# A two-layer spectral mixer and MLP: folded row halves, permuted weights in the second layer, w4 in the order table, and table loads on another queue

## The chip, the cores and the metric

The kernel runs on one core of one Trainium2 chip. The metric is the device time of one execution in microseconds (us). In this kernel TensorE does the matmuls, into banks of the memory called PSUM; ScalarE and VectorE copy and combine the results into the on-chip memory SBUF; GpSimd computes small statistics; SyncE issues loads and stores. All executions compared here are fast (mean granted TensorE clock 0.99 to 1.0). A profile gives the span of one execution, mostly 1.7 to 2.0 us shorter than its time; positions below are us from the start of the span. Line numbers (L403) belong to the kernel whose profile is shown, so the same instruction has another number in the changed kernel.

## The reference, cut to what matters

```python
def A(x):                      # spectral layer, x is [2048, 512]
    X = rfft2(x) * (w_r + 1j * w_i)
    return irfft2(X).astype(bfloat16)

def B(x):                      # mixer and MLP
    h  = gelu(layernorm(x) @ w1)
    hs = concat(h's four column groups, shifted by -1, +1, -2, +2 rows) @ w2
    x1 = x + hs
    return x1 + gelu(layernorm(x1) @ w3) @ w4

x = x + A(layernorm(x));  x = x + B(layernorm(x))     # layer 1
x = x + A(layernorm(x));  x = x + B(layernorm(x))     # layer 2
```

The transforms are matrix products with tables. In each layer: a transform over row groups ("front", into V), a forward DFT over columns (d), one over rows (q), the weighting (p, z), and the inverse steps b, D and P; then w1, w2, w3, w4.

## The kernel before

Each letter of the order table calls one small function; `d4` runs `over_d(4)`, `t4` runs `take_d(4)`, and so on. A schedule is thus a string, and in the timelines every engine runs its own instructions in that order. The code is cut, and `...` marks a cut.

```python
def over_p(K, qs):                      # front: rows' halves added and subtracted by TensorE
    ...
            K.nc.tensor.matmul(o, lhsT=K.x[:, q, a:a + P], rhs=Tq[:, 0:1].to_broadcast([P, 2, P]), start=True, stop=False)
            K.nc.tensor.matmul(o, lhsT=K.x[:, q, z:z + P], rhs=Tq[:], start=False, stop=True)

def take_d(u):                          # t: PSUM -> TV, every second element written
        copy_act(K, tv[u][:].rearrange("p n (e f h) -> p n h e f", e=2, h=2),
                 ps.pop(("d", u)).rearrange("p n (h e f) -> p n h e f", e=2, h=2))

def take_q(u):                          # x: PSUM -> X, two buffers
        X[u] = K.stream.tile([P, 2, 512], BF16, name="X", bufs=2)
        copy_act(K, X[u][:, 0:len(UNITS[u])], ps.pop(("q", u)))

def weigh(u):                           # p: two products on VectorE
    ...
            nc.vector.tensor_tensor(t[:, 0:n], x, w, op=ALU.mult)

def weigh2(u):                          # z: difference and sum on VectorE
        nc.vector.tensor_tensor(z[:, :, 0], a[:, :, 0], b[:, :, 1], op=ALU.subtract)
        nc.vector.tensor_tensor(z[:, :, 1], a[:, :, 1], b[:, :, 0], op=ALU.add)

def take_b(b, eng):                     # m: PSUM -> M, on VectorE ("V") or ScalarE ("A")
```

The 16 column blocks are taken as six pairs and four single units. PSUM has two banks for d, two for q and four for b during this stage. The w4 rows, the layer-norm statistics for layer 2 and the front of layer 2 were issued by plain loops after the order table.

## Time and profile before

| | value | where it is read |
|---|---|---|
| time | 384.94 us, median of 4 (384.69 to 385.62) | the runs |
| span | 383.4 us | the page's first line |
| TensorE's streaming time, from columns | 345.6 us | worked out in the prediction |
| spectral stage of layer 1, of layer 2 | 27.44, 26.87 us | the windows view |
| end of layer 1's w4 to layer 2's first DFT matmul | 5.55 us | the windows view |

The columns of the windows view are: the window, its length, then for PE, PEld, DVE, ACT and POOL the busy us with the number of instructions in brackets, then the clock, the DMA share and GB/s. I cut it at landmarks, which splits the span into pieces that must add up, so that each later difference has a place.

### The profile page before, as it was taken

To read this page: it belongs to the slowest core of one execution; us is meant where nothing else is said; L and a number is where in the kernel's file an instruction comes from. 1 tells how busy PE (TensorE), PEld (TensorE's weight loads), DVE (VectorE), ACT (ScalarE), POOL (GpSimd) and SP (SyncE) were. 2 spreads that over 40 slices of the span, in tenths; PEclk is the share of its full clock that TensorE was granted. 3 is DMA by queue.
4 is the path that set the end of the run, shared out by engine and by line. 5 is a ranking of instruction groups with operands and counts; after the bars stand their busy time and mean duration, and the time that the engine had idled before them with its cause. 6 is when DMAs were issued, how large, how long until landed. Compare 5 with 4: busy or idle time off the path is not lost.

```text
span 383.4 us, 5555 instructions
## 1 busy us (share of the span) xinstructions
PE 354.7 (93%) x2144; PEld 198.7 (52%) x2144; DVE 184.6 (48%) x461; ACT 214.7 (56%) x327; POOL 67.2 (18%) x162
## 2 busy tenths in 40 slices
PE   0869889999999999999996998999999999999996
PEld 0646678445554444444555676855555444444442
DVE  4829969639730321503743996983873011020122
ACT  5768968976987034051225896988598703405100
POOL 3700008443500010000210000753351000000000
PEclk9999999999999999999999999999999999999999
DMA  7945940000000000000000000000000000010011
GB/s 266 328 119 124 358 137 3 0 2 1 3 0 2 0 0 2 0 0 2 0 3 0 0 2 0 2 3 1 2 0 2 0 27 29 0 41 15 27 41 44
DMA packets 12666, 15.17 MB, mean 40 GB/s; under 512 B 1120, under 2 KB 10336, under 8 KB 12640
## 3 DMA queue, kind: packets, MB, share of 16 engines
q1 hardware_dynamic: 11776, 11.34, 9.4%
q10 hardware_dynamic: 864, 3.47, 2.7%
q8 instruction: 17, 0.28, 0.3%
q14 instruction: 9, 0.07, 0.1%
HBM read 12.71 MB, written 2.10 MB: 39 GB/s over the span
## 4 chain that ended last, share of the span: by engine, by line
PE 80%; ACT 8%; DMA 6%; DVE 3%; issue 1%; SPq 1%; POOL 1%; ACTq 0%; DVEq 0%; POOLq 0%
PE ps L555 25%; PE ps L579 25%; PE ps L518 6%; PE ps L502 6%; PE ps L446 4%; ACT TV L145 3%; PE ps L480 3%; PE ps L434 3%; PE ps L372 3%; DMA W<-in_A_w_r_dram 2%; DMA TL<-tab_TL 2%; DMA x_state<-in_A_x_dram 1%; PE ps L416 1%; ACT X L145 1%; PE ps L417 1%
## 5 line engine op out<-in xcount | busy, mean ns | idle before, releaser
L562 ACT ACTIVATE gT<-ps 128x1024 bf16<-128x1024 f32 x56 | 56.9, 1024 | 77.4 <-PE ps L555 77.2
L579 PE MATMUL ps<-w,gT 128*128 128x512 bf16 x448 | 98.3, 379 | 1.4 <-ACT gT L562 1.4
L555 PE MATMUL ps<-xT,w 128*128 128x512 bf16 x448 | 99.0, 379 | 0.0
L581 DVE TENSOR_TENSOR x_state<-ps,x_state 128x512 bf16<-128x512 f32 x32 | 22.1, 691 | 136.7 <-PE ps L579 136.7
L579 PEld LDWEIGHTS <-gT 128*128 128x128 bf16 x448 | 43.7, 98 | 54.3 <-ACT gT L562 2.4
L555 PEld LDWEIGHTS <-w 128*128 128x128 bf16 x448 | 43.5, 98 | 51.0
L145 ACT ACTIVATE xT<-ps 128x1024 bf16<-128x1024 bf16 x32 | 32.1, 1024 | 9.4 <-PE ps L480 9.4
L208 DVE BATCH_NORM_STATS2 ln_st<-x_state 128x6 f32<-128x512 bf16 x43 | 29.4, 683 | 5.1 <-DMA x_state<-in_A_x_dram 4.6
L526 DVE SCALAR_TENSOR_TENSOR xn<-xn,ln_c,ps 128x512 bf16<-128x512 bf16 x32 | 23.2, 744 | 16.2 <-PE ps L518 15.6
L518 PE MATMUL ps<-w,hT 128*128 128x512 bf16 x128 | 29.5, 379 | 0.1
L502 PE MATMUL ps<-xT,w 128*128 128x512 bf16 x128 | 28.8, 379 | 0.0
L145 ACT ACTIVATE V<-ps 128x1024 bf16<-128x1024 f32 (+1 forms) x13 | 12.0, 977 | 28.1 <-PE ps L276 26.8
L274 PE MATMUL ps<-Tq,x_state 128*128 128x256 bf16 x64 | 16.0, 292 | 12.3 <-DVE Tq L263 11.9
L403 DVE TENSOR_TENSOR Pab<-X,W 128x1024 bf16<-128x1024 bf16 (+1 forms) x40 | 21.6, 579 | 11.6 <-DMA W<-in_A_w_i_dram 6.3
L224 POOL TENSOR_SCALAR ln_mv<-ln_s 128x4 f32<-128x4 f32 (+2 forms) x21 | 6.6, 313 | 116.2 <-ACT junk L219 115.6
L145 ACT ACTIVATE TV<-ps 128x1024 bf16<-128x1024 f32 (+1 forms) x20 | 21.5, 1087 | 6.9 <-PE ps L372 6.9
L219 ACT ACTIVATE junk<-xn 128x512 bf16<-128x512 bf16 x32 | 19.9, 623 | 6.2 <-DVE xn L526 6.2
L372 PE MATMUL ps<-FA,V 128*128 128x256 bf16 x128 | 16.9, 272 | 5.6 <-ACT TV L145 3.0
L233 POOL TENSOR_TENSOR ln_r<-ln_ve,mhalf 128x4 f32<-128x4 f32 (+1 forms) x19 | 18.3, 961 | 13.9 <-DVE ln_ve L232 12.7
L518 PEld LDWEIGHTS <-hT 128*128 128x128 bf16 x128 | 12.3, 98 | 14.2 <-ACT hT L509 0.8
L502 PEld LDWEIGHTS <-w 128*128 128x128 bf16 x128 | 12.3, 98 | 14.0 <-issue 0.3
L145 ACT ACTIVATE Y<-ps 128x1024 bf16<-128x1024 f32 x16 | 15.9, 1021 | 5.8 <-PE ps L434 3.0
(65 smaller groups left out, 436.9 us busy)
## 6 DMA issues: line engine op xcount, KB each, us to landing
w<-in_B_w_dram SPq DMA_DIRECT2D x2, 1792.0 KB, 12.3
x_state<-in_A_x_dram SPq DMA_DIRECT2D x8, 256.0 KB, 5.6
out_dram<-x_state SPq DMA_DIRECT2D x16, 128.0 KB, 1.8
TL<-tab_TL ACTq DMA_DIRECT2D x2, 768.0 KB, 7.1
TR<-tab_TR ACTq DMA_DIRECT2D x2, 768.0 KB, 7.8
w<-in_B_w_dram SPq DMA_DIRECT2D x2, 512.0 KB, 5.1
W<-in_A_w_r_dram SPq DMA_DIRECT2D x12, 64.0 KB, 2.7
W<-in_A_w_i_dram SPq DMA_DIRECT2D x12, 64.0 KB, 2.3
```

Of the source, the lines that this page charges most:

```text
L145: K.nc.scalar.activation(dst, src, ACT.Copy, bias=0.0, scale=1.0)
L208: v.bn_stats(st[:], src)
L219: K.nc.scalar.activation(junk[:], src, ACT.Square, bias=0.0, scale=1.0, accum_out=self.s[:, i, 1:2])
L372: nc.tensor.matmul(o[:, i, (1 - h) * 256:(2 - h) * 256], rhs=K.FA[:, t, h], lhsT=V[:, 2 * t + h, b].rearrange("d q c -> d (q c)"), start=( ...
L403: nc.vector.tensor_tensor(t[:, 0:n], x, w, op=ALU.mult)
L502: nc.tensor.matmul(o[:, i], lhsT=K.w1[:, t, j * P:(j + 1) * P], rhs=xT[g][:, t, :], start=(t == 0), stop=(t == 3))
L518: nc.tensor.matmul(o, lhsT=K.hT[:, j, st:st + P], rhs=K.w2[:, j, :], start=(j == 0), stop=(j == 3))
L526: nc.vector.scalar_tensor_tensor(xn[:, q, :], xn[:, q, :], ln[q // 4].c[:, q % 4:q % 4 + 1], ps.pop(("u", n)), op0=ALU.mult, op1=ALU.add, ...
L555: nc.tensor.matmul(o[:, i], lhsT=K.w3[:, c, t * P:(t + 1) * P], rhs=xT3[g][:, c, :], start=(c == 0), stop=(c == 3))
L562: nc.scalar.activation(gT[g][:, 2 * j:2 * j + 2, :], ps.pop(("w", k)), ACT.Gelu_apprx_tanh, bias=0.0, scale=1.0)
L579: nc.tensor.matmul(o, lhsT=gT[g][:, t, i * P:(i + 1) * P], rhs=K.w4[:, t, :], start=(t == 0), stop=(t == 13))
L581: nc.vector.tensor_tensor(K.x[:, q, :], o, K.x[:, q, :], op=ALU.add)
```

## The change

Its intent: take columns off TensorE, cheapen ScalarE's copy in the second spectral stage, fill TensorE's stalls by a finer order, and get the weights in sooner. The core of the diff:

```diff
-    loads = {5: ("TL", slice(0, 8)), 8: ("TR", slice(0, 8)), 11: ("TL", slice(8, 16)), 14: ("TR", slice(8, 16))}
+    loads = {5: ("TL", slice(0, 8)), 8: ("TR", slice(0, 8))}
 ...                                     # load_all, after the first half of W on SyncE
+        if lo == 0:
+            K.load_q("TL", slice(8, 16), nc.sync)
+            K.load_q("TR", slice(8, 16), nc.sync)
 ...
+def over_p_plain(K, qs):                 # front for five of the pairs of rows
+        for t in range(4):
+            K.nc.tensor.matmul(ps[:, i, t * P:(t + 1) * P], lhsT=K.x[:, q, t * P:(t + 1) * P], rhs=Tq[:, 0], start=True, stop=True)
+def fold_V(K, qs, ps, right):            # right: the right halves, copied to SBUF by ScalarE
+    for h, op in ((0, ALU.add), (1, ALU.subtract)):
+        for t in range(2):
+            K.nc.vector.tensor_tensor(v[:, h, t], left[:, t], right[:, t], op=op)
 ...
+        if last:
+            copy_act(K, tv[u][:], src)   # layer 2: folded order, a plain copy
+        else:
+            copy_act(K, tv[u][:].rearrange("p n (e f h) -> p (n e) h f", e=2, h=2), src.rearrange(...))
+def permute(k):                          # weights to folded order, 8 times, in layer 1's order
+        nc.vector.tensor_copy(tw.rearrange("p b (h f) -> p b h f", h=2), w.rearrange("p b (f h) -> p b h f", h=2))
+        nc.vector.tensor_copy(w, tw)
 ...                                     # G is loaded again, with permuted rows, between the layers
-    for op in ORDER.split():             # then loops for w4 and the front
+    for op in (ORDER_B if last else ORDER_A).split():   # w4, its addition, statistics, stores and the front are letters too
```

Less visible: both order tables are new throughout, the spectral part included, and m13 moved from ScalarE to VectorE. The order also moves one pair of the front's rows from ahead of layer 1's last w4 row to behind it. The second step of the layer-norm statistics is issued in a batch, and d's columns stand in another order in PSUM.

## The prediction

> **What bounds the kernel now.** I read the page's busy shares first, then the chain of work that ended last, then the busy time of each engine between landmarks that I took from that chain, and last the timeline around each place where TensorE stood still.
>
> ```profile
> PE 354.7 (93%) x2144; PEld 198.7 (52%) x2144; DVE 184.6 (48%) x461; ACT 214.7 (56%) x327; POOL 67.2 (18%) x162
> ...
> PE 80%; ACT 8%; DMA 6%; DVE 3%; issue 1%; SPq 1%; POOL 1%; ACTq 0%; DVEq 0%; POOLq 0%
> ```
>
> TensorE carries 80% of the chain. Its 93% is inflated, since pipelined matmuls overlap in the record. The chain gives the real pitch: "16 L555 in 3.45 us" is 0.216 us for 512 columns, and 16 transposes of 128 columns in 0.89 us are 0.0556 us each. I counted columns. The groups with 512 columns (L555 448, L579 448, L518 128, L502 128, L390 32) are 1184 matmuls. Those with 256 (L372, L446 and L434 at 128 each; L274, L276, L416, L417 at 64; L388, L389 at 32) are 704, or 352 units of 512. The 256 transposes are 64. So 1600 units at 0.216 us, 345.6 us of the 383.4. Only the 38 us in which TensorE does not stream can go, unless columns go.
>
> Where they lie comes from the windows view, cut at landmarks: first forward-DFT matmul (21.58 in layer 1, 206.15 in layer 2), first inverse-DFT matmul (49.02, 233.02), first w3 (96.79, 279.66), w4 (124.76, 307.63), end of w4 (200.62, 379.93). The columns are window, length, then busy us of PE, PEld, DVE, ACT, POOL.
>
> ```profile
> 21.58:49.02 27.44, 22.96 (x177) 16.91 (x177) 20.72 (x47) 22.68 (x30) 0.00 (x0) 1.00 0.67 204
> 49.02:96.79 47.77, 47.07 (x337) 29.40 (x338) 34.09 (x93) 38.78 (x74) 19.93 (x50) 1.00 0.06 21
> 124.76:200.62 75.86, 75.86 (x369) 36.05 (x370) 26.61 (x62) 18.21 (x18) 5.60 (x9) 1.00 0.00 1
> 200.62:206.15 5.53, 3.55 (x32) 2.88 (x30) 4.27 (x9) 2.43 (x3) 0.55 (x1) 1.00 0.00 0
> 206.15:233.02 26.87, 22.84 (x177) 16.97 (x177) 20.72 (x47) 22.70 (x30) 0.00 (x0) 1.00 0.00 1
> ```
>
> Each spectral stage needs 96 units, 20.7 us, and takes about 27. The w3/w4 stretches are full. The boundary between the layers (200.62 to 206.15) is a serial chain. These lines of the DVE timeline show what paces the spectral stage:
>
> ```profile
> 210.86 0.76 DVE L403 TENSOR_TENSOR Pab<-X,W 128x512 bf16<-128x512 bf16 x2 [4.76 <-ACT X L145]
> ...
> 213.87 1.28 DVE L403 TENSOR_TENSOR Pab<-X,W 128x1024 bf16<-128x1024 bf16 x2
> 215.19 0.42 DVE L409 TENSOR_TENSOR Z<-Pab 128x512 bf16<-128x512 bf16 x1
> 215.53 0.42 DVE L410 TENSOR_TENSOR Z<-Pab 128x512 bf16<-128x512 bf16 x1
> 216.23 1.29 DVE L403 TENSOR_TENSOR Pab<-X,W 128x1024 bf16<-128x1024 bf16 x2 [0.29 <-ACT X L145]
> ...
> 231.59 1.28 DVE L425 CAST M<-ps 128x512 bf16<-128x512 f32 x2
> ```
>
> The reader is to see that VectorE waits 4.76 us for its first X and then hardly stops until the last M. A pair of units costs it 2.0 us (two products, two sums, starts at 213.87 and 215.87), plus 0.6 for each M copy. So this stage is a late start plus 20 us of VectorE, not ScalarE's, though ScalarE is busier in sum. And each layer has one stall before w4:
>
> ```profile
> 306.35 0.59 PE L579 MATMUL ps<-w,gT 128*128 128x512 bf16 x2
> 307.63 2.55 PE L579 MATMUL ps<-w,gT 128*128 128x512 bf16 x11 [0.68 <-ACT gT L562]
> ```
>
> **What the Trainium skill says.** TensorE: Matmul & The Clock Gate, section "Wait — 56ns, not 53.3ns?": warm matmuls start every N ÷ 2.4 GHz plus about 2.5 ns, 55.6 ns at 128 and 215.7 at 512. The trace agrees (0.0556, 0.216). Halved columns are really half the time. VectorE: DVE Perf Modes, section "The perf-mode tier table": a tensor_tensor with a PSUM operand runs at one element per cycle; its errata section gives (N+151)/0.96 ns for fp32. The 512-element add from PSUM (L581) takes 691 ns, as that says; a fold of 256 elements should take 424. ScalarE: Activation LUTs, section "What ACT_TABLE_LOAD costs": 186 + 0.833·N ns, with back-to-back overlap of about 93. That is 1039 for N = 1024; X takes 1012, so it agrees, but TV, the same size written with every second element skipped, takes 1318, which the page doesn't have. DMA: Bandwidth & Descriptors, section "Issuing engines are not separate DMA queues": a second issuer saves only issue time. Here an issue costs SyncE 0.55 to 0.60 us and ScalarE 0.33.
>
> **The change part by part.**
>
> 1. Row halves folded on VectorE. For five of the pairs of rows ahead of layer 2 the sum and difference of the halves no longer come from TensorE (four 256-column matmuls per row) but from four of 128 columns, then an add and a subtract. Ten rows times 4 × (0.109 − 0.0556) = −2.15 us, in a stretch where TensorE has no gap: full value. VectorE gets 20 folds at some 0.35 pitch (0.42 less overlap), 7 us, and loses two casts (1.8). It was busy in 12 of the 19 us from 187 to 206, so it fits, if tightly.
>
> 2. The boundary. Before, 5.53 us from the last w4 to the first DFT matmul. In the new order the last row (E = end of w4) is: add to E+0.7, statistics to 1.65, GpSimd about 0.9 meanwhile one fold set to 3.0, table Tq 3.3, matmuls 3.9, ScalarE copy 4.5, while VectorE folds again to 4.65 and copies the last quarter by 5.05. So 5.05: −0.5. The TensorE work in this gap (3.4 us) is as before.
>
> 3. Layer 2's TV in folded order, with the weights permuted and G reloaded to match. TV becomes a plain copy: 6 × (1.32 − 1.02) + 4 × (0.74 − 0.61) = 2.3 us off ScalarE. Most of it is off the path. What counts is when VectorE starts its stream of pairs: before at 213.87 − 206.15 = 7.7 us. With the d–TV cycle at 1.03 + 1.02 instead of 1.03 + 1.32, three cycles in front, and the order starting d1 t1 d0 q1, I get x2 at T+7.0. From there VectorE has 6 pairs (12.25), two single units (2.35) and M copies (6.5 × 0.6 = 3.9, one more than before): 18.5, to T+25.5; D at about T+25.6 against 26.87: −1.25.
>
> 4. Weight permutation: eight pairs of copies of 1024 elements. The strided one at one element per cycle, as the 1024 CAST took 1.22 us, the plain one at perhaps 0.45: 1.7 each, 13.5 us in all, laid over the MLP of layer 1, where VectorE is busy 34 of 48 and 36 of 104 us. I count 0.
>
> 5. w4 in the order table. w4 rows now stand among w3 blocks, so TensorE doesn't run into the last gelu. The gap is 307.63 − 306.35 − 2 × 0.216 = 0.85 us in each layer: −1.7. Similarly three D blocks are issued before the first P, which had waited 0.24 for Y: −0.5 for both.
>
> 6. TL, TR second halves on SyncE, behind W's first half. Before, W's second plane landed at 27.5, and VectorE waited 6.3 us for it in two places; the second one held it at 27.60 when X had been ready at 26.7. The 1.5 MB ahead of W at about 330 GB/s are 4.6 us, and the shared completion semaphores made SyncE wait for TL and TR (2.3 + 1.5). I expect W by 22 to 23, ahead of the first product at about 24. But the d–TV cycle is unchanged in this layer (1.32), so the stream of pairs starts at T+7.8, against T+8.7 with the wait, and with one M copy more I get D at T+26.5 against 27.44. T itself hardly moves: statistics are batched (bn before aggr), but GpSimd's square-root chain ends at 15.39 and the tables start at 15.42. ScalarE no longer waits to issue (0.8 + 1.3), also off this path. Sum −1.0. W's second half (16 issues × 0.6 from about 22, some waits) lands near 35, its first use is at T+15, 36: just in time.
>
> The output tail is unchanged: one add, one store. Sum: −2.15 − 0.5 − 1.25 − 1.7 − 0.5 − 1.0 = −7.1: 385.05 − 7.1 = 377.95, so 378.0.
>
> **The rivals.** (a) ScalarE is the bound of the spectral stages (22.7 of 26.9 us busy). For it: the d–TV–d cycle is visible, 2.45 us each. Then part 3 would pay 2.3 us and the total be 377. Against it: VectorE has gaps of only some 1.1 us after 213. (b) VectorE becomes a bound at the boundary: 3 us of add, fold and statistics per 3.02 us of w4 row. Folds or permutations that run later than thought hold PSUM banks, and TensorE waits; each such slip costs 0.5 to 1.5 us, giving 379 to 380.5. For it: the fold order leaves it no slack in the last two rows. (c) W's second half comes late, since TL and TR now stand in SyncE's queue in front of it and 16 issues take 9.6 us: 1 to 2 us back, 379.5. For it: my margin is 1 us. (d) The new orders also remove stalls in the MLP that I left: layer 1 spends 47.77 us from D to w3 where layer 2 spends 46.64, and the count of columns says 45.8. If half of the 2.9 us goes, 376.5.
>
> **Range and chances.** The removed columns and the two gelu gaps (3.85 us) are near certain. The rest, 3.25 us, is scheduling, which could double or vanish. Range 375.6 to 380.6. Two per cent is 377.35, just below my figure, so faster has 0.40, within 0.59, slower 0.01: slower would need a new wait of 15 us.
>
> **What would show it.** TensorE 10 units fewer, all ahead of layer 2; TV of layer 2 at 1.02; first w4 without a gelu wait; the boundary near 5 us; the two spectral stages near 25.6 and 26.5; no wait of a product for W. Wrong, if the spectral stage of layer 2 shrinks by the whole 2.3 us (ScalarE was its bound) or not at all, if TensorE waits for folds, or if a product waits for W near 36.

## The result, and the profile after

The changed kernel takes 379.45 us (median of 4, 379.04 to 381.04) against 384.94. The ratio is 0.9862, 95% interval 0.9831 to 0.9893: the same at the 2% mark, and inside the range given. A ratio is the mean time of one kernel's fast runs over that of the other's fast runs of the same rounds, so not quite the ratio of the medians quoted.

The page of the changed kernel, busy shares and the chain:

```profile
PE 352.1 (93%) x2144; PEld 197.3 (52%) x2144; DVE 193.4 (51%) x493; ACT 212.0 (56%) x327; POOL 64.7 (17%) x166
...
PE 79%; DMA 6%; DVE 5%; ACT 4%; SPq 3%; issue 1%; POOL 0%; ACTq 0%; DVEq 0%
```

These averages say little. VectorE does 9 us more, and TensorE's share is as before. The windows tell where the time went. First the pieces of the kernel before which the prediction did not show, cut 0.02 us earlier at the end of w4:

```profile
49.02:200.60 151.58, 150.20 (x867) 79.08 (x868) 70.06 (x182) 79.51 (x121) 31.07 (x69) 1.00 0.02 7
200.60:206.15 5.55, 3.57 (x32) 2.90 (x30) 4.27 (x9) 2.43 (x3) 0.55 (x1) 1.00 0.00 0
...
233.02:379.90 146.88, 145.94 (x832) 75.84 (x832) 53.81 (x135) 74.07 (x116) 25.48 (x60) 1.00 0.04 14
379.90:383.40 3.50, 0.00 (x0) 0.00 (x0) 0.69 (x1) 0.00 (x0) 0.00 (x0) 0.84 0.11 37
```

The same pieces of the changed kernel:

```profile
21.25:49.01 27.76, 22.95 (x176) 16.98 (x177) 21.29 (x48) 22.70 (x29) 0.00 (x0) 1.00 0.77 243
49.01:196.96 147.95, 147.58 (x859) 77.46 (x860) 78.91 (x208) 76.89 (x120) 30.27 (x72) 1.00 0.03 10
196.96:202.25 5.29, 3.68 (x40) 2.90 (x38) 4.75 (x14) 4.01 (x6) 0.77 (x2) 1.00 0.00 0
202.25:228.08 25.83, 22.64 (x176) 16.91 (x177) 21.31 (x48) 20.75 (x29) 0.00 (x0) 1.00 0.00 1
228.08:373.80 145.72, 145.72 (x832) 75.93 (x832) 52.88 (x135) 73.98 (x116) 23.56 (x60) 1.00 0.04 14
373.80:377.70 3.90, 0.00 (x1) 0.00 (x0) 0.69 (x1) 0.00 (x0) 0.00 (x0) 1.00 0.10 36
```

| piece | before | forecast | changed |
|---|---|---|---|
| start to first DFT matmul, layer 1 | 21.58 | 21.5 | 21.25 |
| spectral stage, layer 1 | 27.44 | 26.5 | 27.76 |
| inverse DFT to end of w4, layer 1 | 151.58 | 148.3 | 147.95 |
| end of w4 to first DFT matmul, layer 2 | 5.55 | 5.05 | 5.29 |
| spectral stage, layer 2 | 26.87 | 25.6 | 25.83 |
| inverse DFT to end of w4, layer 2 | 146.88 | 145.8 | 145.72 |
| last addition and store | 3.50 | 3.5 | 3.90 |
| span | 383.4 | 376.3 | 377.7 |

The forecast column is the prediction's own terms put into these pieces: 148.3 is 151.58 less 2.15 (columns), 0.85 (gelu gap) and 0.24 (Y). Six pieces are within 0.4 us of the forecast; of the first, little can be said, since over the profiles of these kernels it varies from 21.25 to 22.35. One is not: layer 1's spectral stage did not get shorter by 1.0 but longer by 0.3. VectorE's timeline of that stage in the changed kernel:

```profile
28.93 1.28 DVE L443 TENSOR_TENSOR Pab<-X,W 128x1024 bf16<-128x1024 bf16 x2
...
36.57 0.68 DVE L443 TENSOR_TENSOR Pab<-X,W 128x1024 bf16<-128x1024 bf16 x1
37.58 0.69 DVE L443 TENSOR_TENSOR Pab<-X,W 128x1024 bf16<-128x1024 bf16 x1 [0.33 <-DMA W<-in_A_w_i_dram]
...
47.99 0.69 DVE L465 CAST M<-ps 128x512 bf16<-128x512 f32 x1 [0.66 <-PE ps L457]
```

The stream of pairs starts at 28.93 − 21.25 = 7.7 us, as forecast (7.8). But it then takes until 48.68, 19.75 us instead of 18.5: one product waits 0.33 for the second half of W, and the last M waits 0.66 for its matmul. That matmul had itself waited for a bank which ScalarE had to empty, as TensorE's timeline shows:

```profile
47.29 0.27 PE L456 MATMUL ps<-TR,Z 128*128 128x256 bf16 x1 [0.97 <-ACT M L149]
```

The wait for W suggests rival (c) of the prediction, W's second half late behind TL and TR. SyncE's waits in the changed kernel (total, times, longest) seem to confirm it:

```profile
SPq L178 <- DMA TR<-tab_TR: 3.5, 2, 2.8
SPq L178 <- DMA TL<-tab_TL: 1.5, 1, 1.5
```

SyncE stood still for 2.8 us before a part of W because it had to wait for TR to land. So I had two theories for the lost 1.0: the loads (A), or the order of the stage's end (B). The experiments tell them apart.

### The profile page after: what moved, and what is told of

Read it like the earlier page. It is cut to its first block, busy times and chain, and to the rows that moved or that the text cites. A ratio compares the mean times of both kernels' runs of the same rounds, so it can differ in the third digit from the quotient of the medians.

```text
span 377.7 us, 5575 instructions
## 1 busy us (share of the span) xinstructions
PE 352.1 (93%) x2144; PEld 197.3 (52%) x2144; DVE 193.4 (51%) x493; ACT 212.0 (56%) x327; POOL 64.7 (17%) x166
## 4 chain that ended last, share of the span: by engine, by line
PE 79%; DMA 6%; DVE 5%; ACT 4%; SPq 3%; issue 1%; POOL 0%; ACTq 0%; DVEq 0%
PE ps L598 26%; PE ps L611 25%; PE ps L561 7%; PE ps L545 6%; DMA TR<-tab_TR 4%; PE ps L474 4%; PE ps L486 4%; PE ps L523 4%; PE ps L408 2%; DMA x_state<-in_A_x_dram 2%; DVE Pab L443 1%; SPq L178 1%; SPq L177 1%; ACT hT L552 1%; ACT TV L149 1%
## 5 line engine op out<-in xcount | busy, mean ns | idle before, releaser
L611 PE MATMUL ps<-w,gT 128*128 128x512 bf16 x448 | 99.6, 379 | 0.0
L605 ACT ACTIVATE gT<-ps 128x1024 bf16<-128x1024 f32 x56 | 56.0, 1025 | 76.1 <-PE ps L598 75.7
L216 DVE BATCH_NORM_STATS2 ln_st<-x_state 128x6 f32<-128x512 bf16 x43 | 28.6, 684 | 4.9 <-DMA x_state<-in_A_x_dram 4.6
L232 POOL TENSOR_SCALAR ln_mv<-ln_s 128x4 f32<-128x4 f32 (+2 forms) x21 | 5.8, 276 | 134.5 <-ACT junk L227 134.0
L286 PE MATMUL ps<-Tq,x_state 128*128 128x256 bf16 x44 | 11.8, 305 | 11.2 <-DMA x_state<-in_A_x_dram 9.7
L149 ACT ACTIVATE TV<-ps 128x1024 bf16<-128x1024 f32 (+1 forms) x20 | 19.2, 973 | 5.2 <-PE ps L408 5.1
L244 POOL TENSOR_SCALAR ln_ve<-ln_mv 128x4 f32<-128x4 f32 (+1 forms) x19 | 4.8, 251 | 79.8 <-DVE ln_mv L237 78.6
L552 ACT ACTIVATE hT<-ps 128x512 bf16<-128x512 f32 x32 | 17.3, 605 | 1.5 <-PE ps L545 1.5
```

The costliest lines, as they stand in the source:

```text
L149: K.nc.scalar.activation(dst, src, ACT.Copy, bias=0.0, scale=1.0)
L216: self.K.nc.vector.bn_stats(st[:], src)
L552: nc.scalar.activation(hv[:, 2 * h + i, 4 * g:4 * g + 4, 1:P + 1], o[:, i].rearrange("p (q c) -> p q c", q=4), ACT.Gelu_apprx_tanh, bias=0 ...
L605: nc.scalar.activation(gT[g][:, 2 * j:2 * j + 2, :], ps.pop(("w", k)), ACT.Gelu_apprx_tanh, bias=0.0, scale=1.0)
L611: nc.tensor.matmul(o, lhsT=gT[g][:, t, i * P:(i + 1) * P], rhs=K.w4[:, t, :], start=(t == 0), stop=(t == 13))
```

## The experiments

Each kernel is the changed kernel with the edit shown; diffs are cut, and remarks after # are mine. Times of one batch are compared with runs of the kernel before in the same batch, whose medians were 386.1 to 386.2 in these three batches against 384.94 with the first: 12 of those 21 runs had a clock of 0.994 or 0.995 and took 385.9 or more, and all but one of the others took 384.6 to 385.6. So ratios of these batches look about 0.3% better than the first one's, and are not compared with it. The start up to the first DFT matmul varied from 21.4 to 22.4 us between them, so stages are compared by length.

**e1: TL and TR back on ScalarE.**

```diff
-        if lo == 0:
-            K.load_q("TL", slice(8, 16), nc.sync)
-            K.load_q("TR", slice(8, 16), nc.sync)
-    loads = {5: ..., 8: ...}
+    loads = {5: ..., 8: ..., 11: ("TL", slice(8, 16)), 14: ("TR", slice(8, 16))}
```

> The changed kernel with the second halves of TL and TR issued by ScalarE again (part 6 undone). In the changed kernel the first DFT matmul of layer 1 is at 21.25 and the first inverse-DFT matmul at 49.01, where I had forecast 48.0. Theory (the move does help, by getting W's first half in early): W's first half lands near 27.5 again, the first products wait for it, the stream of pairs on VectorE starts about 1 us later (28.93 -> 29.9), first inverse-DFT matmul 49.5 to 50.0, time +0.7. Rival (what W's first half gains, its second half gives back, since TL and TR now stand ahead of it): inverse-DFT start within 0.3 of 49.01, time within 0.3 of the changed kernel.

Measured: 380.09 us (ratio 0.9841). First DFT matmul 21.70, first inverse-DFT matmul 49.08, so the stage took 27.38. The theory fell: not 49.5 or more. The rival held for the position (its time is 0.6 above the changed kernel's, with a start 0.45 later and a tail 0.4 longer). VectorE's first wait is put down to W here, but it is as long (3.36 us) as the wait for X in the changed kernel, so W came hardly later than X would have let it start: in this order the earlier W is worth nothing at the end of the stage.

**e2: TR's second half after W's second half.**

```diff
-        if lo == 0:
-            K.load_q("TL", slice(8, 16), nc.sync)
-            K.load_q("TR", slice(8, 16), nc.sync)
+        K.load_q("TL" if lo == 0 else "TR", slice(8, 16), nc.sync)
```

> The changed kernel with TR's second half issued after W's second half instead of ahead of it; it is first needed near 41 us. In the changed kernel SyncE stood still from 27.2 to 29.9 for TR to land, and a product waited at 37.58 for W. Theory A (the late second half of W ate the 1.0 us that I had forecast for layer 1's spectral stage): inverse-DFT start 48.0 to 48.4, time -0.8. Theory B (the wait for W was 0.33 us, and the rest was lost at the end of the stage, where ScalarE's copies of M come late because ScalarE stands in front of an X that waits for its buffer): inverse-DFT start 48.6 to 48.8, time -0.3. If TR itself comes late, a matmul waits for it near 41 and the time rises.

Measured: 379.82 us (ratio 0.9833); 21.81 to 49.19, again 27.38. Theory A fell: three load orders, and the inverse DFT starts at 49.0 to 49.2 in each; by length the stage is 0.38 shorter than in the changed kernel's profile, which is theory B's size. How much of that the loads cost can be seen in e3, e4, e7 and e13 below, which have the changed kernel's loads and its order in layer 1: their stage takes 27.37 or 27.38 and no product waits for W. So the wait of 0.33 cost 0.4 us in the one profiled execution, which had started 0.4 us earlier than these, and nothing in the others; the rest of the lost 1.0 is not the loads'.

**e3: no folds.**

```diff
-PLAIN = 5
+PLAIN = 0          # and the five folds' VectorE letters dropped from ORDER_A
```

> The changed kernel with the five pairs of rows ahead of layer 2 computed as before (sum and difference on TensorE, one copy of 128x1024 on ScalarE), no folds on VectorE. Theory: 10 units of 512 columns come back on TensorE. 1.3 us of them before the end of layer 1's w4 and 0.86 in the gap behind it, where VectorE's second fold (1.4 us) held the last copy: end of w4 196.97 -> 198.3, start of layer 2's DFT 202.25 -> 203.0 to 203.6, time +1.0 to +1.6. Prediction as it was written: +2.15. Rival (folds hold up TensorE through VectorE as much as they save): within 0.4.

Measured: 381.37 us (ratio 0.9872). The windows view of e3, same pieces:

```profile
49.19:198.42 149.23, 148.86 (x858) 78.44 (x859) 75.05 (x196) 78.16 (x120) 30.13 (x72) 1.00 0.02 7
198.42:203.91 5.49, 4.36 (x40) 3.66 (x38) 2.31 (x6) 4.54 (x6) 0.77 (x2) 1.00 0.00 0
203.91:229.63 25.72, 22.65 (x177) 16.93 (x178) 21.33 (x48) 20.76 (x29) 0.00 (x0) 1.00 0.00 1
```

In this new order the folds are worth 149.23 − 147.95 = 1.28 before the end of w4 and 0.20 in the gap, 1.48 together, not 2.15. Three of the five pairs stand ahead of the last w4 row, 6 rows × 4 × (0.109 − 0.0556) = 1.28: full value, as TensorE is the path there. The other two (0.86) are in the gap, where the chain through addition, statistics and the last copies sets the end, and only 0.20 of them shows. The traces also show what the edit does not undo: 32 of the front's matmuls stood ahead of layer 1's last w4 matmul in the kernel before, and 24 do in the changed kernel and here. The order has moved two rows into the gap, 8 × 0.109 = 0.87 us, and so even without folds this piece is 151.58 − 149.23 = 2.35 shorter than before.

**e4: layer 2's TV strided again, no permutation, G not reloaded.**

```diff
-        if last:
-            copy_act(K, tv[u][:], src)
-        else:
+        if True:
             copy_act(K, tv[u][:].rearrange("p n (e f h) -> p (n e) h f", e=2, h=2), ...)
-        if not last: K.load_G2()          # and the eight permute letters dropped
```

> The changed kernel with part 3 and 4 undone: layer 2's TV written with stride again (1.32 us instead of 1.02), weights not permuted, G not reloaded. Theory (VectorE paces the spectral stage; a shorter TV only moves the start of its stream): layer 2's spectral stage, now 202.25 to 228.08 = 25.83, becomes 26.6 to 27.1, time +0.7 to +1.2. Rival (ScalarE paces it): 28.1, time +2.3. The permutations gone from layer 1 give back nothing.

Measured: 381.73 us (ratio 0.9912, with one run of four at 385.39 and a clock of 0.99). Layer 2's stage, and who VectorE waited for in it:

```profile
202.28:229.92 27.64, 22.86 (x177) 17.00 (x177) 21.42 (x48) 22.59 (x29) 0.00 (x0) 1.00 0.00 1
```

```profile
DVE Pab L441 <- ACT X L147: 5.6, 6, 3.2
DVE M L463 <- PE ps L455: 0.7, 1, 0.7
```

27.64 against 25.83: 1.81, between theory and rival. And 27.64 is longer than the 26.87 of the kernel before, which had the same strided TV. VectorE waits for X six times here, the longest of 3.2 at the start, the others in the stream. From inverse DFT to end of w4, layer 1 without the eight permutations takes 147.94 (49.04 to 196.98), with them 147.95: they cost nothing, as forecast. The longer stage points at the new order of the spectral stage.

**e8: the old order for the spectral stages of both layers.**

```diff
-ORDER_A = "d1 d0 t1 q1 t0 x1 d2 p1 ... b14 m12A m14A" + rest
-ORDER_B = "d1 t1 d0 q1 t0 d2 x1 p1 ... b14 m11V m14A" + rest
+          "d0 d1 t0 t1 q0 d2 t2 q1 d4 x1 p1 x0 ... b14 m14A" + rest   # in both
```

> The changed kernel with the spectral part of both order tables (all up to the first inverse-DFT matmul) in the order of the kernel before; everything else, the loads and the plain TV of layer 2 too, as changed. So far, layer 1's stage from first DFT to first inverse-DFT matmul takes 27.4 us with three different load orders (W is not what holds it), layer 2's takes 25.83 with the plain TV and 27.64 with the strided one, and before it took 26.87 with the strided one. Theory C (the new order itself is worse wherever TV is strided, because it puts more of the M copies late and behind ScalarE's X): layer 1 becomes 26.4 to 26.9, layer 2 becomes 26.0 to 26.5. Theory D (layer 1 is held by something that both orders share): layer 1 stays at 27.2 to 27.5.

Measured: 379.14 us (ratio 0.9825, 0.9805 to 0.9844). The two stages, then VectorE's waits in layer 2's:

```profile
21.41:48.28 26.87, 22.70 (x174) 16.98 (x178) 20.76 (x47) 22.70 (x30) 0.00 (x0) 1.00 0.84 257
201.51:227.23 25.72, 22.41 (x174) 16.86 (x177) 20.46 (x47) 20.89 (x30) 0.00 (x0) 1.00 0.00 1
```

```profile
DVE Pab L443 <- ACT X L149: 4.9, 1, 4.9
DVE M L465 <- ACT M L149: 0.3, 1, 0.3
```

Theory C held for layer 1, at the edge: it falls to 26.87, which is to the hundredth what layer 2 took before. For layer 2 its forecast (26.0 to 26.5) was missed, since with the plain TV the old order is no slower than the new one (25.83, and 25.72 in e3). In layer 1 the loads are no limit any more, and what it had lost to them (27.44 − 26.87 = 0.57) is regained. The old order has one M copy fewer on VectorE (47 instructions against 48). TensorE's b matmuls, which waited 1.8 us for ScalarE's M in the changed kernel's layer 1 (first line; 1.5 in e7), wait for none in e8's, only for VectorE's Z:

```profile
PE ps L456 <- ACT M L149: 1.8, 2, 1.0
PE ps L456 <- DVE Z L449: 0.6, 1, 0.6
```

In the old order, layer 2 went from 26.87 to 25.72 by the plain TV alone, 1.15 us, and here VectorE, after its first X, waits once for 0.3 us. That is the picture the prediction drew (VectorE paces, 1.25). In layer 2's new order it holds as long as TV is plain, and fails with the strided one.

**e6: the two new orders exchanged.**

```diff
-ORDER_A = spectral_A + rest_A ; ORDER_B = spectral_B + rest_B
+ORDER_A = spectral_B + rest_A ; ORDER_B = spectral_A + rest_B
```

> The spectral parts of the two new order tables exchanged: layer 1 runs in layer 2's order and the other way round. If the two orders differ only in detail and TV's stride sets the length: layer 1 stays at 27.3 to 27.7 (as layer 2 did with strided TV, 27.64), layer 2 at 25.7 to 26.0. If layer 1's own order is what cost it the forecast 1.0: layer 1 falls to 26.5.

Measured: 380.74 us (ratio 0.9863). Layer 1 in B's order 27.60 (27.38 in its own); layer 2 in A's order 26.67 (25.83 in its own). The first version held for layer 1 and missed layer 2; the second missed. With e4 and e8 every order has now run with both forms of TV:

| order of the spectral stage | TV strided | TV plain |
|---|---|---|
| the kernel before's | 26.87 (layer 2 before, layer 1 in e8) | 25.72 (layer 2 in e8) |
| ORDER_A's | 27.38 (layer 1 in e1 and others) | 26.67 (layer 2 in e6) |
| ORDER_B's | 27.64 (layer 2 in e4), 27.60 (layer 1 in e6) | 25.83 (layer 2), 25.72 in e3 |

Neither new order beats the old one. Layer 1's own costs 0.5 us with the strided TV and more with the plain one; layer 2's costs 0.8 with the strided TV and at most 0.1 with the plain one.

**e9 and e10: M copies moved between the engines.**

```diff
 # e9                                       # e10
-layer 1: m0A m4A   layer 2: m5V m9V        -layer 1: m5V m9V   layer 2: m0A m4A
+layer 1: m0V m4V   layer 2: m5A m9A        +layer 1: m5A m9A   layer 2: m0V m4V
```

> Two M copies moved: in layer 1 from ScalarE to VectorE (blocks 0 and 4), in layer 2 from VectorE to ScalarE (blocks 5 and 9). An M copy is 0.60 us of VectorE and 0.5 of ScalarE. If VectorE paces both stages (as I had written): layer 1 27.4 -> 28.6, layer 2 25.83 -> 24.7. If ScalarE paces layer 1 (strided TV) and VectorE layer 2: layer 1 26.4 to 27.0, layer 2 24.7 to 25.2. If ScalarE paces both: layer 1 26.4 to 27.0, layer 2 26.5.

> The opposite: in layer 1 two M copies moved from VectorE to ScalarE (blocks 5 and 9), in layer 2 two from ScalarE to VectorE (blocks 0 and 4). VectorE paces both: layer 1 26.2 to 26.6, layer 2 27.0. ScalarE paces layer 1, VectorE layer 2: layer 1 28.0 to 28.4, layer 2 26.8 to 27.1. If the two engines hold each other up through the four banks that wait for M, both directions cost something in both layers.

| | M copies on VectorE | layer 1 | layer 2 |
|---|---|---|---|
| changed kernel's orders (e1, e2; changed kernel) | 7.5 | 27.38 | 25.83 |
| two more on VectorE (e9; e10) | 9.5 | 28.42 | 26.75 |
| two more on ScalarE (e10; e9) | 5.5 | 27.45 | 26.52 |

Times 383.41 us for e9 (ratio 0.9923) and 380.59 for e10 (0.9862); 1.7 us of e9's is its last stretch of matmuls, at a clock of 0.99. Copies added to VectorE lengthen both stages, by 1.04 and 0.92 for 1.2 us of work. Copies taken from it shorten neither: −1.2 us of VectorE gives +0.07 and +0.69. So in these orders neither engine alone paces the stage, and none of my three versions held for both layers. VectorE's waits for X in e9's layer 2 rise from 3.6 us to 5.3, and in e10's layer 1 from 4.4 to 5.3, which fits an M that stands in ScalarE's order ahead of an X and delays it.

**e7: stores right behind their additions.**

```diff
-... A9 y3 W14 y9 ... y4 y14 y10 A8 y1 y15 y12 y8
+... A9 y9 W14 ... A8 y8
```

> The changed kernel with each store right behind its addition in the order. In the changed kernel ten stores leave SyncE between 366.2 and 374.9, since those that were long ready stand behind one that waits, and from the end of the last w4 to the end of the span it takes 4.0 us where the kernel before took 3.67. Theory (stores that crowd at the end hold the last one): the tail falls to 3.6 to 3.7, time -0.3 to -0.4. Rival (the tail varies from run to run by that much anyway): no change beyond 0.2.

Measured: 379.57 us (ratio 0.9843). From the last addition's matmul to the end it takes 3.8 us, against 3.9 and 3.5 before. The theory fell; what lengthened the tail by 0.4 us stays open. In the other runs it took 3.8 to 3.9, twice 4.3 to 4.4.

**e13: w4 of layer 2 where it was before.**

```diff
-... W2 o10 L2 w10 ... W3 o15 U5 ... W0 ...       (layer 2's table likewise: w4 rows among w3 blocks)
+... all w3 of groups 0, 1; W0..W3; w14..w20; W4..W7; w21..w27; W8..W15
```

> The changed kernel with layer 2's w4 rows taken out of the order table and put where the kernel before had them: rows 0 to 3 after all w3 blocks of the first two groups, and so on (part 5 undone in layer 2; layer 1 as changed). Theory: the gelu gap before the first w4 comes back, 0.85 us: first inverse-DFT matmul to end of w4 145.56 -> 146.4, time +0.85. Rival (the stall was hidden elsewhere, or the interleaving has a cost of its own): within 0.3.

Measured: 380.69 us (ratio 0.987). Inverse DFT to end of w4 is 374.80 − 228.40 = 146.40 in place of 145.72: 0.68 for w4 in the table, near the forecast 0.85. But the wait is another one than I had named, for the edit does not restore the old neighbours of w4. TensorE's timeline of e13 where w4 begins:

```profile
300.11 1.06 PE L523 MATMUL ps<-ident,x1n 128*128 128x128 bf16 x16
301.66 0.62 PE L523 MATMUL ps<-ident,x1n 128*128 128x128 bf16 x8 [0.50 <-DVE x1n L268]
302.12 12.25 PE L611 MATMUL ps<-w,gT 128*128 128x512 bf16 x56
```

The first 56 w4 matmuls run on without a gelu wait, because the last transposes stand between; instead TensorE waits 0.5 us for VectorE's x1n. So this run shows that the place of w4 matters, but it does not measure the gelu wait of the kernel before.

**e11 and e12: a version to beat both.** e11 is e8 with e7's stores; e12 moves layer 2's m5 to ScalarE as well.

```diff
 # e12 against e11, layer 2's spectral part
-d12 t12 p6 z6 m5V p8
+d12 t12 p6 z6 m5A p8
```

> The kernel with the old spectral order in both layers (which took 26.87 and 25.72, 379.14) and the stores early. If the stores' crowding is real: 378.8. It is the base of a version that may beat both.

> As the one before, and in layer 2 the M copy of block 5 on ScalarE. In the old order VectorE has no wait between its first pair and the last M of layer 2. If VectorE paces: layer 2's stage 25.72 -> 25.1, time -0.6. If ScalarE's in-order row holds an X back in turn, as the moves in the new order showed (+0.7): 25.7 to 26.3.

Measured: e11 379.12 us (0.9829, 0.9804 to 0.9853), e12 379.17 (0.9835); the 378.8 did not come. Layer 2's stage was 25.72 in e11 and 25.81 in e12: even in the old order, where VectorE hardly waits after its first X (0.3 us, in e12 some 0.8), one M less for it brings nothing. So "VectorE paces" is too short there as well: in e8's layer 2 ScalarE's and VectorE's last M copies end together, at 227.08, 0.15 us before the inverse DFT starts. e8 and e11 are the best versions. In one batch, and with the same stores, e11 takes 379.12 where e7 takes 379.57. The gain over the changed kernel is the 0.5 us in layer 1's stage; the 0.1 in layer 2's is no more than the new order itself varied in e3.

## Why the prediction was right or wrong

The total was right: 378.0 forecast, 379.45 measured, inside the range and of the class given the higher chance. The sum of terms was 7.1, the span fell by 5.7, of which 0.3 is an earlier start, which is chance. Of the 1.4 us missing, 1.26 are layer 1's spectral stage in this profile (0.87 in others). Two figures are slightly off: 2.15 should be 2.14, and the 2.9 of rival (d) 2.8. By its steps:

1. *Folds, −2.15.* Ahead of the end of layer 1's w4 TensorE did lose this much, but not by the route written: 1.28 by the folds of six rows and 0.87 by the two rows that the order moved into the gap. The folds themselves are worth 1.48 (e3). The step "in a stretch where TensorE has no gap: full value" is true of three pairs, not of the two that I myself had placed in the serial gap in part 2. A fold took 412 ns, where the prediction had estimated 424 from the page's formula:

```profile
L310 DVE TENSOR_TENSOR V<-ps,right 128x256 bf16<-128x256 f32 x20 | 7.0, 412 | 1.3 <-ACT right L149 1.3
L660 DVE COPY Pab<-W 128x1024 bf16<-128x1024 bf16 x8 | 5.4, 679 | 0.0
L661 DVE COPY W<-Pab 128x1024 bf16<-128x1024 bf16 x8 | 3.4, 427 | 0.3
```

2. *Boundary, −0.5.* 5.29 for 5.05. The chain ran as listed up to VectorE's last copy, which was done 4.8 us after the end of w4; but ScalarE's last copy came 0.4 us behind it, not half a microsecond ahead. Rival (b), folds that hold banks and stall TensorE, did not come: no such wait is in its list.

3. *Layer 2's TV, −1.25.* −1.04 measured. TV does take 1.02 now, and VectorE's stream started at 209.35 − 202.25 = 7.1 us, forecast 7.0. It lasted to 227.94, 18.6 us, where VectorE's work had been summed to 18.5:

```profile
209.35 1.29 DVE L443 TENSOR_TENSOR Pab<-X,W 128x1024 bf16<-128x1024 bf16 x2
...
226.66 1.28 DVE L465 CAST M<-ps 128x512 bf16<-128x512 f32 x2
```

So this step was right, the wait at the start and the sum behind it. But e4, e6 and e8 show that the new order had no part in the gain. The plain TV alone, in the old order, gives 1.15, and in the new order 1.81, because the new order is 0.8 worse with a strided TV.

4. *Permutations, 0.* Right: 147.94 without and 147.95 with them (e4). They were also cheaper than thought, 0.68 + 0.43 us each in the lines above, not 1.7.

5. *w4 in the table, −0.85 in each layer, and Y, −0.24.* Right. In layer 2 1.16 in all, forecast 1.09. In layer 1 the piece fell by 3.63, of which 1.28 are folds and 0.87 the moved rows, so 1.48 against 1.09. These waits of TensorE in the kernel before (both layers) have no entry in the changed kernel's list:

```profile
PE ps L579 <- ACT gT L562: 1.4, 2, 0.7
PE ps L446 <- ACT Y L145: 0.5, 2, 0.2
PE ps L480 <- DVE xn L256: 0.4, 1, 0.4
```

The first two are those that the prediction named. The third, in layer 1, about covers the 0.4 that it had not: that much of rival (d), stalls of the MLP that the new order removes, came true. No experiment separates it.

6. *Loads and layer 1's spectral stage, −1.0.* This is the step that failed. W's first half came in time, as forecast: in the changed kernel no first product waits for it. The tables on SyncE then held W's second half up by 2.8 us, as rival (c) feared, and one of the prediction's own signs of being wrong came true: a product waited for W, at 37.3. But that cost 0.4 us, in this one execution; without it the stage still takes 27.38 instead of 26.5 (e1 to e4, e7, e13). What failed is the term "18.5 us of VectorE from the start of the stream". I summed VectorE's work and took it as the length of the stream in the new order. In layer 2, with the plain TV, it was; in layer 1, with the strided one, the stream took 19.75, and 19.35 in e7 (29.70 to 49.05). With the old order put back (e8) the stage takes 26.87, which is −0.57 and about half of what I had expected; there the stream takes 18.95 (29.18 to 48.13), with 0.8 of waits in it. So the order, with its choice of engine for m13, is shown to cost 0.5 of the missing 0.9. What in it does so is seen but not isolated: near the end the b matmuls wait for banks that ScalarE's M copies have yet to empty, and VectorE's last M waits for them. The M copy that the new order adds to VectorE is not it alone, for with two taken off (e10) the stage takes 27.45. Rival (a), ScalarE as the bound, would have given 2.3 for the plain TV; measured are 1.15 or 1.81, so it isn't the whole truth either.

7. *Tail, 0.* +0.4, open.

## What to carry to other kernels

When engines pass tiles along in fixed orders, the sum of one engine's work is a lower bound and not the length: here it met layer 2's stream to 0.1 us and missed layer 1's by 0.9. Test an order apart from the change that came with it, since the old order of one stage beat the new one by 0.5 us while the rest of the change won. Columns removed from TensorE count where TensorE is the path and hardly in a serial gap, so split such a gain by place before adding it up; and work moved into such a gap can be nearly free, as two rows were here. And a load moved away from one queue can stop the next one in line through a completion it must wait for; look at the end of the stage, not at the first wait that vanished.

## What the Trainium skill lacked or had wrong

- ScalarE: Activation LUTs, section "What ACT_TABLE_LOAD costs", gives 186 + 0.833·N ns and names no pattern of access. A copy of 1024 elements from PSUM that writes every second element took 1.32 us, the plain one 1.02 (the page's formula: 1.04).
- VectorE: DVE Perf Modes, section "The perf-mode tier table", gives four elements per cycle for a bf16 tensor_scalar in SBUF and does not set apart scalars that are read per partition. Here 512 elements took 407 ns (two per-partition fp32 scalars) and 256 took 278 (one): 0.50 ns per element, two per cycle at the page's 0.96 GHz. The plain bf16 copy did reach the page's rate for four, 1024 elements in 427 ns, and the strided one that for two, 679.
- DMA: Bandwidth & Descriptors, section "Issuing engines are not separate DMA queues", calls the issue time "usually small relative to the DMA itself". For the pieces of W, most of 64 KB, an issue held SyncE mostly 0.55 to 0.62 us, with 2.3 to 5.9 us to landing, and 34 such pieces make some 20 us of issuing; the page has no figure for how long a whole issue holds its engine.
- No page says that a stage can get longer when work is taken off one of its engines: moving two copies of M from VectorE to ScalarE (1.2 us) lengthened layer 2's stage by 0.69 us, to 26.52, with no engine busy for more than 22.4 of them.
